# First token block of a retention and ELU layer kernel: whole-chunk products on half arrays, reordered loads, two layer tiles by chunks

## The chip, the cores and the metric

The kernel runs on one core of a Trainium2 chip. The core has a matrix engine, TensorE (PE in the profile, with PEld for its weight loads), three elementwise engines, VectorE (DVE), ScalarE (ACT) and GpSimd (POOL), and a queue engine, SyncE (SP), which issues the DMA transfers here. Each engine works through its own instructions in order, and semaphores tie them together. PE writes into PSUM[...]; everything else lies in SBUF. The metric is the time of one execution on the device in microseconds (us). A profile's span is what lies between the first and the last instruction of the program's own.

## What is computed

```python
gamma = 1.0 - 2.0 ** (-5.0 - np.arange(H))          # H = 8 heads, D = 64, S = 768, B = 4
for t in range(S):
    state = gamma[None, :, None, None] * state + np.einsum('bhd,bhe->bhde', k[:, :, t], v[:, :, t])
    y[:, :, t] = D ** -0.5 * np.einsum('bhd,bhde->bhe', q[:, :, t], state)
x = y.transpose(0, 2, 1, 3).reshape(B * S, H * D)   # 3072 tokens x 512
h = x @ w_in                                        # 512 x 2048
g = np.where(h > 0.0, h, np.exp(np.minimum(h, 0.0)) - 1.0)
out = g @ w_out                                     # 2048 x 512
```

All is fp32. The weights arrive as 64-bit numbers and are turned into fp32 on the chip.

## The kernel before

The 3072 tokens are worked through in six blocks of 512. A block goes through retention (`q`, `k`, `v` to `x`), the first layer with its ELU, and the second layer. Later blocks use a form of Strassen's scheme for both layers; the first block computes its first layer plainly (`plain_first`), because the weights are still arriving.

**Retention.** A block has four chunks of 128 tokens. One load (`load`, 1 MB, L99) brings a chunk: `q` and `k` turned so that channels lie on partitions, and `k` and `v` with tokens on partitions. `scale_v` (L275) multiplies `v` by a power of gamma for each token. Before the change, each chunk is treated as two sub-chunks of 64 tokens: `score_products` (L302) makes `k` times `q` for each sub-chunk and head as 64x64x64 products, which occupy a quarter of the PE array each; a mask on DVE (`mask_pair` L324, or in `scores` L312) cuts them to the causal triangle and stores them over `k`; `state_products` (L332) makes the sum of `k` times `v` of each sub-chunk, and `state_sum` (L343) adds it to the running state; `within` (L389) multiplies the masked scores by `v`; `across` (L399) adds the state times `q`. At the end DVE multiplies by powers of gamma (`etab`, made by ACT in `powers_of`, L246) into the block's input `xb`. The first two chunks are issued one at a time (`outputs_of_first`, L414), the third and fourth as a pair (L1155 to L1166).

**Weights.** Sixteen pieces of 1 MB come in through three staging buffers (`load_piece_parts`, L130). Piece 2n is `w_a[n]`, piece 2n + 1 is `w_b[n]`, for four values of n; the others are the second layer's. `prepare` (L147) reads a piece with ACT: the low words (L164), the top byte (L166), and the high words scaled (L168), unless DVE does this last one (L190). `decode` (L180) then joins them on DVE (L191, L194). A piece can be handled in two halves. When a piece is decoded, `load_piece` issues the load that takes over its buffer. `hold` (L112) makes one load wait for another through a copy of one element on POOL, which the load must follow.

**The layer.** `plain_first` (L489) makes sixteen tiles of 128 features by 512 tokens, four products each. Tiles 4n and 4n + 1 use `w_a[n]`, 4n + 2 and 4n + 3 use `w_b[n]`. Tiles 0 to 4 are made in two halves of 256 tokens, since the second half of `xb` is ready later (tile 0's first half again in two parts of 128); the others in one. They use PSUM banks a, a, b, d in turn, and tile 4 one of the pool that retention uses. Each tile ends in `elu` (L472): two ACT operations (L477, L478) and one on DVE (L481), which is issued one tile later.

**Order.** There is no scheduler: the Python order is the order on each engine. The head of the program, L1108 to L1171, is written out by hand. `unread` (L1104) issues products whose result nothing reads. `take` advances the decoding of the current piece by one step, `next(inner)` issues the next piece of `plain_first`. From L1187 on, a loop over the remaining steps of `plain_first` attaches other work to step n: loads of the next block's chunks, `next_piece` (decode one, prepare the next), the next block's retention from n = 10 on.

Of the kernel before, what the change touches and what calls it, by code (L numbers as in the profile page):

```python
# [18 lines left out]
def kernel(  # L19
# [127 lines left out]
    def prepare(parts=1, by_vector=False, between=None):  # L147

        n = len(prepared)
        if n >= NPIECE:  # L150
            return
        t = staged[n]
        if n < 2 * NQ:
            dst = (w_a, w_b)[n % 2][n // 2].rearrange("p a b c d -> p (a b c d)")
        else:

            dst = w_s[n % NQ].rearrange("p a b c d -> p (a b c d)")[:, 0:1024]
        todo = []
        for part in range(parts):
            if part and between:  # L160
                between()
            c = slice(part * 1024 // parts, (part + 1) * 1024 // parts)
            lo, hi, flat = t[:, c, 0], t[:, c, 1], dst.bitcast(U32)[:, c]
            nc.scalar.activation(flat, lo, AF.Copy, scale=2.0**-29)  # L164
            top = dst.bitcast(F8).rearrange("p (c b) -> p c b", b=4)[:, c, 3]
            nc.scalar.activation(top, hi.bitcast(FP32), AF.Copy, scale=2.0**-120, saturate=False)  # L166
            if not by_vector:
                nc.scalar.activation(lo.bitcast(FP32), hi.bitcast(FP32), AF.Copy, scale=2.0**-112)  # L168
            todo.append((lo, flat, hi if by_vector else None))
        prepared.append((dst, todo))  # L170
# [83 lines left out]
    parts = load_piece_parts(2)  # L254
    next(parts)
    load(1)
    next(parts, None)
    load_piece()
    load(2)
    load(3)  # L260
    load_piece(staged[1][:, :, 0].bitcast(FP32))
# [25 lines left out]
    def state(tb, n):  # L287

        if n % (2 * CPB) == 0:
            return carry[(tb + n // (2 * CPB)) % 2]  # L290
        if (tb, n) == (0, 3):

            return xt[0].rearrange("p a t -> p (a t)")[:, 0:256].rearrange("p (h e) -> p h e", e=D)

        k = raw[tb * CPB + (n - 1) // 2][1][:, 0].rearrange("p h d -> p (h d)")
        return k[:, (n - 1) % 2 * 256 : ((n - 1) % 2 + 1) * 256].rearrange("p (h e) -> p h e", e=D)
# [5 lines left out]
    def score_products(sc, tb, pp, x):  # L302
        qk = raw[tb * CPB + 2 * pp + x][0]
        for p in range(HP):
            for sub in range(2):
                for a in range(2):
                    nc.tensor.matmul(  # L307
                        sc[a][rows(sub), x, p, :], lhsT=qk[rows(a), 1, p, rows(sub)],
                        rhs=qk[rows(a), 0, p, rows(sub)], start=True, stop=True, skip_group_check=True,
                    )  # L310

    def scores(tb, pp):  # L312

        sc = [ps_r.tile([P, 2, HP, D], FP32, name="sc", tag="r") for _ in range(2)]
        for x in range(2):
            score_products(sc, tb, pp, x)
        for a in range(2):
# [4 lines left out]
            )  # L322

    def mask_pair(sc, x):  # L324

        place = raw[x][0][:, 1].rearrange("p h c -> p (h c)").rearrange("p (a n t) -> p a n t", a=2, t=D)
        for a in range(2):
            nc.vector.tensor_tensor(
                out=place[:, a], in0=sc[a][:, x], in1=cmask.unsqueeze(1).to_broadcast([P, HP, D]), op=ALU.mult
            )  # L330
# [12 lines left out]
    def state_sum(kvs, tb, pp, x, sub, copy=None):  # L343
# [3 lines left out]
        if fresh(tb, n):  # L347
            (copy or nc.scalar.copy)(state(tb, n + 1), kvs[sub][:, x])
# [65 lines left out]
    def outputs_of_first():  # L414

        y = [bank(x).rearrange("p a (b x d) -> p (a b) x d", b=2, x=2) for x in "bd"]
        for x in range(2):
            for j in range(4):
                pt = raw[x][0][:, 1].rearrange("p h c -> p (h c)")
                within(0, 0, x, j, y, lambda p: pt[:, ((j // 2) * HP + p) * D :][:, 0:D])  # L420
            yield
            across(0, 0, x, 0, y)
            for sub in range(2):
                if not fresh(0, 2 * x + sub):
                    seen = epool.tile([P, 8], FP32, name="seen", tag="seen")
                    nc.vector.tensor_copy(seen[:, 0:4], y[sub][:, :, x, 0])
            if x:
                yield
            across(0, 0, x, 1, y)
            if x:  # L430
                yield
            for sub in range(2):
                nc.vector.tensor_tensor(
                    out=place_of(xb[:, :, 0 : 2 * C])[:, :, x, sub, :], in0=y[sub][:, :, x],
                    in1=place_of(powers[:, :, 0 : 2 * C])[:, :, x, sub, :], op=ALU.mult,
                )
            if not x:
                yield
# [50 lines left out]
    def plain_first():  # L489
# [12 lines left out]
        for k in range(5):  # L502
            hp = bank("aabd"[k]) if k < 4 else ps_r.tile([P, 2, TH], FP32, name="hp", tag="r")
            banks.append(hp.rearrange("p a b -> p (a b)"))
            if k == 0:
                part(0, slice(0, C))
                yield
                part(0, slice(C, 2 * C))
            else:
                part(k, half[0])  # L510
            if k:
                yield
        for k in range(5):
            part(k, half[1])
            n, w, row, fi = tiles[k]
            elu(g_plain[row * NF + 2 * n + fi], banks[k])
            yield
        for k, (n, w, row, fi) in enumerate(tiles[5:]):
            hp = bank("aabd"[k % 4]).rearrange("p a b -> p (a b)")
# [589 lines left out]
    for n in range(28):  # L1109
# [4 lines left out]
    sc = [ps_r.tile([P, 2, HP, D], FP32, name="sc", tag="r") for _ in range(2)]  # L1114
    score_products(sc, 0, 0, 0)
    scale_v(0)
    mask_pair(sc, 0)
    unread(1, TH)
    kvs = [ps_r.tile([P, 2, HP, D], FP32, name="kv", tag="r") for _ in range(2)]
    state_products(kvs, 0, 0, 0, range(2))  # L1120
    state_sum(kvs, 0, 0, 0, 0, nc.vector.tensor_copy)
    y = outputs_of_first()
    next(y)
    next(y)
    unread(1, TB)
    score_products(sc, 0, 0, 1)
    state_sum(kvs, 0, 0, 0, 1)
    prepare(2, between=lambda: powers_of(slice(2 * C, S)))
    piece = decode(True)
    take()  # L1130
    take()
    scale_v(1)
    mask_pair(sc, 1)
    inner = plain_first()
    next(inner)
    state_products(kvs, 0, 0, 1, range(2))
    state_sum(kvs, 0, 0, 1, 0)
    next(y)
    next(y)
    next(y)  # L1140
    unread(1, TB)
    next(y, None)
    take()
    take()
    take()
    state_sum(kvs, 0, 0, 1, 1)
    prepare(2, by_vector=True)
    next(inner)
    piece = decode()
    take()  # L1150
    take()
    scale_v(2, True)
    scale_v(3, True)
    next(inner)
    scores(0, 1)  # L1155
    states(0, 1)
    take()
    prepare(2)
    piece = decode(True)
    take()  # L1160
    next(inner)
    y = outputs(0, 1)
    next(y)
    next(y)
    take()
    next(y, None)  # L1166
    next(inner)
    take()
    take()
    take()  # L1170
    prepare()  # L1171
# [15 lines left out]
    for n, _ in enumerate(inner):  # L1187
# [4 lines left out]
        if n in (1, 2, 4, 5, 7, 9):  # L1192
            next_piece(n in (1, 2, 5, 7))
# [294 lines left out]
```

## Time and profile before

| what | value |
|---|---|
| time, median of 3 runs | 632.84 us (632.33 to 633.2) |
| time of the profiled execution | 632.87 us |
| its span | 630.9 us |
| PE busy | 624.8 us, 99% |
| DVE busy | 483.1 us, 77% |
| ACT busy | 253.3 us, 40% |
| POOL busy | 21.8 us, 3% |
| mean traffic | 217 GB/s; 403 GB/s from 5.15 to 11.6 us |

A row of the timeline has the start in us, the length in us, engine, line, operation, output and inputs, shape and count, and in brackets how long the engine was idle and what ended that. For PE, 64*64 or 128*128 is the part of the array that is used and 128x512 the output; one fp32 product is two records, so x8 is four products. The ends of PE's records are modelled, so starts are compared. A row of the wait list has who waited for whom, the total in us, how often, and the longest. Chunk loads and piece loads are issued at L110 and L142.

### The profile page before, as it was taken

What the parts mean: (1) busy time and instruction counts of PE and PEld (TensorE: products, weight loads), DVE (VectorE), ACT (ScalarE), POOL (GpSimd) and SP (SyncE); (2) the same over time, 40 slices, a digit from 0 to 9 for tenths busy, and PEclk for the clock granted to TensorE, in tenths of its full rate; (3) what the DMA queues carried; (4) which work ended last, traced back from release to release, by engine and by line L of the source; (5) the groups of instructions that cost most, each with busy time, mean ns of one, the idle gap of its engine ahead of it and who ended that gap; (6) DMA issues with size and microseconds to landing.
All of it is one profiled execution on the core that took longest, in us unless ns stands there. A gap on an engine that the chain in (4) does not pass through costs nothing.

```text
span 630.9 us, 16128 instructions
## 1 busy us (share of the span) xinstructions
PE 624.8 (99%) x6680; PEld 560.1 (89%) x6680; DVE 483.1 (77%) x884; ACT 253.3 (40%) x472; POOL 21.8 (3%) x25
## 2 busy tenths in 40 slices
PE   8999999999999999999999999999999999999998
PEld 5864578888899999889999989999988999988997
DVE  5779789989789675699685588777489877558975
ACT  6698635015541114653112646111465211366311
POOL 1021000000000000200000200000110000000000
PEclk9999999999999999999999999999999999999999
DMA  8698669689287888405888702888810798600794
GB/s 331 278 406 291 188 210 268 196 267 316 81 311 248 239 255 299 180 2 174 274 266 292 282 2 64 264 284 296 310 73 12 216 308 252 217 18 2 232 309 162
DMA packets 75897, 136.85 MB, mean 217 GB/s; under 512 B 6320, under 2 KB 31792, under 8 KB 70704
## 3 DMA queue, kind: packets, MB, share of 16 engines
q1 hardware_dynamic: 75824, 135.82, 64.8%
q8 instruction: 53, 0.87, 0.5%
q14 instruction: 20, 0.16, 0.1%
HBM read 114.56 MB, written 21.23 MB: 215 GB/s over the span
## 4 chain that ended last, share of the span: by engine, by line
PE 77%; SPq 1%; DVE 1%; DMA 1%; issue 0%; ACT 0%; ACTq 0%; DVEq 0%
PE pa L955 20%; PE pa L913 10%; PE pd L955 10%; PE pb L955 5%; PE pa L867 5%; PE pb L913 4%; PE pa L740 4%; PE qa L913 3%; PE pd L867 2%; PE qd L913 2%; PE pd L913 2%; PE pd L740 2%; PE y L394 1%; PE sc L307 1%; PE y L409 1%; PE kv L338 1%
## 5 line engine op out<-in xcount | busy, mean ns | idle before, releaser
L963 ACT COPY ms<-pa 128x128 f32<-128x128 f32 x104 | 27.7, 266 | 146.7 <-PE pa L955 146.7
L955 PE MATMUL pa<-ts,wq 128*128 128x128 f32 x560 | 74.2, 275 | 0.0
L955 PE MATMUL pd<-ts,wq 128*128 128x128 f32 x552 | 73.5, 276 | 0.0
L955 PEld LDWEIGHTS pa<-ts,wq 128*128 128x128 f32 x560 | 68.5, 192 | 0.4
L955 PEld LDWEIGHTS pd<-ts,wq 128*128 128x128 f32 x552 | 67.1, 192 | 0.6 <-DVE res L967 0.2
L955 PE MATMUL pa<-gC,wq 128*128 128x128 f32 x480 | 64.7, 278 | 0.0
L478 ACT ACTIVATE r<-r 128x512 f32<-128x512 f32 x96 | 60.5, 630 | 3.1
L955 PEld LDWEIGHTS pa<-gC,wq 128*128 128x128 f32 x480 | 59.0, 192 | 1.5 <-issue 0.3
L477 ACT ACTIVATE r<-gC 128x512 f32<-128x512 f32 x64 | 39.9, 624 | 32.4 <-DVE gC L921 32.4
L967 DVE TENSOR_TENSOR res<-pd,ms 128x128 f32<-128x128 f32 x68 | 19.5, 287 | 39.6 <-PE pd L955 38.4
L481 DVE SCALAR_TENSOR_TENSOR gC<-r,gC 128x512 f32<-128x512 f32 x64 | 44.0, 719 | 0.7 <-ACT r L478 0.7
L829 DVE TENSOR_TENSOR ts<-gC,ts 128x512 f32<-128x512 f32 x60 | 41.3, 688 | 1.0
L829 DVE TENSOR_TENSOR ts<-gC 128x512 f32<-128x512 f32 x60 | 41.0, 684 | 0.0
L281 POOL TENSOR_TENSOR chunk<-chunk,vf 128x512 f32<-128x512 f32 x16 | 20.0, 1251 | 428.8 <-DMA chunk<-in_qkv_dram 345.8
L955 PE MATMUL pb<-gC,wq 128*128 128x128 f32 x240 | 31.7, 275 | 0.0
L988 ACT COPY res<-pa 128x128 f32<-128x128 f32 x34 | 9.0, 266 | 55.0 <-PE pa L955 55.0
L955 PEld LDWEIGHTS pb<-gC,wq 128*128 128x128 f32 x240 | 29.2, 192 | 0.0
L690 ACT COPY m<-pa 128x512 f32<-128x512 f32 x24 | 13.9, 581 | 30.2 <-PE pa L740 16.3
L921 DVE TENSOR_TENSOR gC<-qa,gC 128x512 f32<-128x512 f32 x8 | 5.5, 692 | 25.0 <-PE qa L913 18.3
L913 PE MATMUL pa<-xt,w_b 128*128 128x256 f32 x96 | 23.0, 382 | 0.0
L913 PE MATMUL pa<-xt,w_s 128*128 128x256 f32 x96 | 23.0, 382 | 0.0
L913 PE MATMUL pa<-xb,w_a 128*128 128x256 f32 x96 | 22.7, 379 | 0.0
(255 smaller groups left out, 1244.3 us busy)
## 6 DMA issues: line engine op xcount, KB each, us to landing
wq<-scratch_dram SPq DMA_DIRECT2D x277, 256.0 KB, 4.3
chunk<-in_qkv_dram SPq DMA_DIRECT2D x23, 1024.0 KB, 8.6
wraw<-in_w_dram SPq DMA_DIRECT2D x15, 1024.0 KB, 6.0
out_dram<-res SPq DMA_DIRECT2D x14, 256.0 KB, 3.8
scratch_dram<-gT SPq DMA_DIRECT2D x12, 256.0 KB, 4.3
scratch_dram<-m SPq DMA_DIRECT2D x12, 192.0 KB, 6.0
scratch_dram<-so SPq DMA_DIRECT2D x4, 512.0 KB, 4.6
scratch_dram<-wi SPq DMA_DIRECT2D x2, 1024.0 KB, 6.4
```

The costliest lines, as they stand in the source:

```text
L281: eng.tensor_tensor(out=kv[:, 1], in0=kv[:, 1], in1=vf[:, i].unsqueeze(2).to_broadcast([C, H, D]), op=ALU.mult)
L477: nc.scalar.activation(e, h, AF.Relu, scale=-1.0)
L478: nc.scalar.activation(e, e, AF.Exp, scale=-1.0)
L481: nc.vector.scalar_tensor_tensor(g, e, -1.0, h, ALU.add, ALU.max)
L690: nc.scalar.copy(m, ps)
L740: nc.tensor.matmul(ps[:, fi, :], lhsT=w[:, fi, j2, :], rhs=x[:, j2, :], start=(begin and fi == 0 and j2 == 0), stop=(j2 == 1), skip_group_ ...
L829: sub = lambda o, x, y: nc.vector.tensor_tensor(out=o, in0=x, in1=y, op=ALU.subtract)
L867: nc.tensor.matmul(ps[:, f, :], lhsT=lhs[f], rhs=xs[j][k], start=(begin and f == 0), stop=True, skip_group_check=True,)
L913: nc.tensor.matmul(ps[:, fi, :], lhsT=w[:, fi, j2, :], rhs=x[:, j2, :], start=(j in (1, 7) and fi == 0 and j2 == 0), stop=(j2 == 1), skip_ ...
L955: nc.tensor.matmul(ps, lhsT=w[:, f, :], rhs=ts[j][k][:, f, :], start=(begin and f == 0), stop=(f == 3), skip_group_check=True,)
L963: nc.scalar.copy(m, ps)
L967: nc.vector.tensor_tensor(out=o, in0=x, in1=y, op=ALU.add)
```

## The change

Four things are different in the first block. The rest of the program is the same, line for line.

- Its four chunks are handled whole. `whole_scores` makes `k` times `q` of 128 by 128 tokens with 64 channels, on the upper or lower half of the array; `whole_mask` masks them against the full triangle on DVE, one mask for each row half, the second result going to a buffer of its own; `whole_products` and `whole_within` contract over all 128 tokens and write 64 rows, on the left or right half of the array; `whole_across` uses quarters, with 128 columns. All four chunks go through the same functions, one at a time, and there is one state per chunk.
- The loads stand in another order: chunk 0 in two halves, chunk 1, piece 0 in two halves, chunks 2 and 3, piece 1, piece 2 (held behind piece 1). Before it was chunk 0 in halves, piece 0's first half, chunk 1, piece 0's second half, piece 1, chunks 2 and 3, piece 2 (held).
- In `plain_first`, tiles 0 and 1 are made in four parts of 128 tokens each, between the chunks' retention; tiles 2 to 15 are made whole. The bank order is a, a, then d, b, a, a in turn.
- The head of the program is written anew. The unread products of 256 and 512 columns between the chunks are gone (the first stays, with 29 small ones instead of 28). Of the weights, pieces 0 and 1 are prepared in the head, in halves, and piece 2 at step n = 0 of the loop; before, pieces 0 to 3 were. POOL scales chunks 2 and 3 instead of DVE. In `prepare`, the scaled high words come second instead of third. The powers for later tokens (`powers_of`, four ACT operations) stand behind both halves of piece 0 instead of between them.

```diff
-    parts = load_piece_parts(2)
-    next(parts)
     load(1)
-    next(parts, None)
-    load_piece()
+    for _ in load_piece_parts(2):
+        pass
     load(2)
     load(3)
-    load_piece(staged[1][:, :, 0].bitcast(FP32))
+    load_piece()
...
+    def whole_scores(m):
+        qk = raw[m][0]
+        sc = [ps_r.tile([P, HP, C], FP32, name="sc", tag="r") for _ in range(2)]
+        for p in range(HP):
+            for a in range(2):
+                nc.tensor.matmul(
+                    sc[a][:, p, :], lhsT=qk[rows(a), 1, p, :], rhs=qk[rows(a), 0, p, :],
+                    start=True, stop=True, skip_group_check=True,
+                )
+        more = hpool.tile([P, TB], FP32, name="pt", tag="h")
+        whole[m] = sc, (qk[:, 1], more.rearrange("p (h c) -> p h c", c=C))
+
+    def whole_mask(m, a):
+        sc, pt = whole[m]
+        nc.vector.tensor_tensor(
+            out=pt[a], in0=sc[a], in1=causal.unsqueeze(1).to_broadcast([P, HP, C]), op=ALU.mult
+        )
+
+    def whole_within(m, y, a):
+        pt, kv = whole[m][1], raw[m][1]
+        for u in range(2):
+            for c in range(2):
+                nc.tensor.matmul(
+                    y[a][rows(c), u, :], lhsT=kv[:, 1, head(a, u, c), :], rhs=pt[a][:, 2 * u + c, :],
+                    start=(u == 0), stop=(m == 0), skip_group_check=True,
+                )
+
+    def whole_across(m, y, a):
+        q = raw[m][0]
+        for u in range(2):
+            for c in range(2):
+                p = 2 * u + c
+                nc.tensor.matmul(
+                    y[a][rows(c), u, :], lhsT=state(0, 2 * m)[rows(a), p, :], rhs=q[rows(a), 0, p, :],
+                    start=False, stop=True, skip_group_check=True,
+                )
+
+    def whole_products(m):
+        kv = raw[m][1]
+        t = ps_r.tile([P, HP, D], FP32, name="kv", tag="r")
+        for p in range(HP):
+            for a in range(2):
+                nc.tensor.matmul(
+                    t[rows(a), p, :], lhsT=kv[:, 0, 2 * p + a, :], rhs=kv[:, 1, 2 * p + a, :],
+                    start=True, stop=True, skip_group_check=True,
+                )
+        return t
+
+    def whole_sum(m, t):
+        if m:
+            nc.vector.tensor_tensor(out=state(0, 2 * m + 2), in0=t, in1=state(0, 2 * m), op=ALU.add)
+        else:
+            nc.scalar.copy(state(0, 2), t)
+
+    def whole_end(m, y, a):
+        c, j = slice(m * C, (m + 1) * C), slice(2 * a, 2 * a + 2)
+        nc.vector.tensor_tensor(out=xb[:, j, c], in0=y[a], in1=powers[:, j, c], op=ALU.mult)
+
+    def whole_outputs(m):
+        y = whole_place()
+        for a in range(2):
+            whole_within(m, y, a)
+            if m:
+                whole_across(m, y, a)
+        return y
...
-        for k in range(5):
-            hp = bank("aabd"[k]) if k < 4 else ps_r.tile([P, 2, TH], FP32, name="hp", tag="r")
...
+        for k in range(2):
+            banks.append(bank("a").rearrange("p a b -> p (a b)"))
+            for x in range(2):
+                part(k, slice(x * C, (x + 1) * C))
                 yield
...
+        for x in (2, 3):
+            for k in range(2):
+                part(k, slice(x * C, (x + 1) * C))
+                if x == 3:
+                    n, w, row, fi = tiles[k]
+                    elu(g_plain[row * NF + 2 * n + fi], banks[k])
                 yield
...
-    for n in range(28):
+    for n in range(29):
...
+    whole_scores(0)
     scale_v(0)
-    mask_pair(sc, 0)
...
+    whole_mask(0, 0)
+    whole_mask(0, 1)
+    scale_v(2)
+    scale_v(3)
+    load_piece(staged[1][:, :, 0].bitcast(FP32))
+    t = whole_products(0)
+    whole_sum(0, t)
+    y = whole_outputs(0)
+    whole_end(0, y, 0)
+    whole_end(0, y, 1)
+    whole_scores(1)
+    prepare(2)
+    piece = decode(True)
+    scale_v(1)
+    whole_mask(1, 0)
+    whole_mask(1, 1)
+    y = whole_outputs(1)
+    t = whole_products(1)
+    whole_end(1, y, 0)
     take()
     take()
+    whole_end(1, y, 1)
+    whole_sum(1, t)
     inner = plain_first()
     next(inner)
+    powers_of(slice(2 * C, S))
+    whole_scores(2)
     next(inner)
+    take(3)
+    whole_mask(2, 0)
+    whole_mask(2, 1)
     next(inner)
+    y = whole_outputs(2)
+    t = whole_products(2)
+    whole_end(2, y, 0)
+    whole_end(2, y, 1)
+    whole_sum(2, t)
+    whole_scores(3)
+    next(inner)
+    whole_mask(3, 0)
+    whole_mask(3, 1)
     prepare(2)
     piece = decode(True)
+    y = whole_outputs(3)
     next(inner)
+    whole_end(3, y, 0)
+    whole_end(3, y, 1)
+    t = whole_products(3)
     next(inner)
+    whole_sum(3, t)
+    take(2)
...
-        if n in (1, 2, 4, 5, 7, 9):
-            next_piece(n in (1, 2, 5, 7))
+        if n == 0:
+            take(3)
+            prepare(2)
+        elif n in (1, 2, 3, 4, 5, 7, 9):
+            next_piece(n in (2, 3, 5, 7))
```

## The prediction

> **What bounds the kernel now.** First the page's busy line, then the wait list of TensorE (PE) for the first 95 us, then the timeline of PE and of whatever released it there.
>
> ```profile
> PE 624.8 (99%) x6680; PEld 560.1 (89%) x6680; DVE 483.1 (77%) x884; ACT 253.3 (40%) x472; POOL 21.8 (3%) x25
> ```
>
> ```profile
> PE pa L1106 <- DVE blank L208: 1.5, 1, 1.5
> PE pd L409 <- DVE seen L426: 0.5, 2, 0.3
> PE kv L338 <- DVE chunk L281: 0.4, 1, 0.4
> PE y L409 <- DVE seen L378: 0.3, 1, 0.3
> PE pa L497 <- DVE w_a L194: 0.2, 1, 0.2
> ```
>
> PE is the bound nearly everywhere: 99% of the span, and after the first 28 us this list has no entry; the same list from 86 us to the end is empty. So what the front of the kernel gains or loses in PE time reaches the end whole, and one number measures it: when the first tile that both kernels issue alike starts. That is tile 5 of the plain layer, the first row of the two below that has 512 columns.
>
> ```profile
> 15.92 3.10 PE L497 MATMUL pa<-xb,w_a 128*128 128x128 f32 x16
> ...
> 20.86 1.16 PE L307 MATMUL sc<-chunk 64*64 64x64 f32 x64
> 21.84 1.11 PE L338 MATMUL kv<-chunk 64*64 64x64 f32 x64
> 22.88 1.99 PE L497 MATMUL pd<-xb,w_b 128*128 128x256 f32 x8
> ...
> 38.21 2.31 PE L521 MATMUL pa<-xb,w_a 128*128 128x512 f32 x5
> 41.65 3.60 PE L521 MATMUL pa<-xb,w_b 128*128 128x512 f32 x8
> 45.08 3.60 PE L521 MATMUL pb<-xb,w_b 128*128 128x512 f32 x8
> ...
> 60.93 3.70 PE L521 MATMUL pb<-xb,w_b 128*128 128x512 f32 x8
> 64.56 2.08 PE L338 MATMUL kv<-chunk 64*64 64x64 f32 x112
> ```
>
> Tile 5 starts at 38.21. From 15.92 on PE runs without a hole; before that it waits for loads and fills itself with products that nothing reads (L1106). Loads land one after the other, and these rows show when:
>
> ```profile
> 8.11 0.68 ACT L164 ACTIVATE w_a<-wraw 128x512 uint32<-128x512 uint32 x1 [2.33 <-DMA wraw<-in_w_dram]
> 10.66 0.56 PEld L307 LDWEIGHTS sc<-chunk 64*64 64x64 f32 x32 [0.85 <-DMA chunk<-in_qkv_dram]
> 15.10 0.17 POOL L115 COPY wraw<-wraw 1x1 f32<-1x1 f32 x1 [12.83 <-DMA wraw<-in_w_dram]
> ```
>
> By place in the SP queue these are the loads that complete 1.5, 2.5 and 4 MB.
>
> **What the Trainium skill says.** "TensorEngine Tiling (Array Packing)", Key Properties: tiles of one mode run side by side, and "Mode switching requires drain". The trace agrees with both. Sixteen 64x64 products with 64 columns start at 12.65 and the next group at 13.16 (0.51 us): four at a time, since one 128-column product on the whole array takes 0.223 (groups of four start at 321.15, 322.05, 322.94). A 512-column tile takes 3.43 among its like (41.65 to 45.08) and 3.63 between two 64x64 groups (60.93 to 64.56): 0.20 for going in and out. The same page lists 64x128 and 128x64 as modes of two tiles; no run here shows either. "TensorE: Matmul & The Clock Gate", Part 1: the array starts at half clock and is released after some 3.4 us of activity. The trace shows it: 32 records of scores take 0.99 (5.15 to 6.14), 32 records of state 0.51 (12.65 to 13.16).
>
> **The change, part by part.** (a) Unread products: four become one large at the start; those at 6.14, 9.51 and 14.96 go (0.9 to 1.1 each). They fill waits, so taking them away gives nothing by itself.
>
> (b) Retention of four chunks. Before, each of its four products per chunk is sixteen 64x64x64 products, 0.47 to 0.51, so about 2.0 per chunk. After, per chunk: scores, eight 64x128 products of 128 columns; within, eight 128x64 of 128 columns; across, eight 64x64 of 128 columns with only the two column halves alternating, so two at a time; state, eight 128x64 of 64 columns. If two run at a time: scores 4 x 0.223 = 0.89, within 0.89, across 0.89, state 0.46 (the present price of 16 products in fours). That is 3.13, 1.1 more per chunk: half of each causal square is computed and masked away. An unseen price is whether pairs run side by side: bounded by 0.89 (all) and 1.79 (none) for scores; I take all, since 64x64 tiles that share rows or columns do it now.
>
> (c) Mode changes. Before, the second pair of chunks costs three excursions. After, within and across alternate for each half array, so a chunk changes mode six or seven times. Price of one segment: 0.20 for a full-array one (above); 64x64 ones with 32 or 64 records show 0.05 to 0.17 over 0.0145 per record (20.86 to 21.84 is 0.98 for 64, that is 0.05; 21.84 to 22.88 is 0.11). I take 0.15 per half-form segment and 0.13 for across; the bounds are 0 and 0.20.
>
> (d) Layer tiles. Five tiles by halves become two by chunks and three whole: the same columns. A 128-column product costs 0.223, so a tile 3.57 instead of 3.43: +0.28 for two.
>
> (e) Loads. Chunk 1 moves ahead of the first weight piece, and chunks 2 and 3 ahead of the second. By megabytes: chunk 0 as now (scores start at 5.15); chunk 1 completes 2 MB, between 8.11 and 10.66, so 9.4; the halves of piece 0 at 2.5 and 3 MB, 10.66 and about 12.6 (ACT takes up the second half of piece 0, now also at 3 MB, at 12.58); chunk 2 at 4 MB, 15.1; chunk 3 at 5 MB, 17.6; piece 1 at 6 MB, about 20.2. Piece 2 is held by the POOL copy until piece 1 is there; from issue to landing takes some 4.8 with the queue empty, so 25.2. SP issues the next load behind it, and POOL has the two scalings in front: neither late.
>
> **The walk.** Chunk 0: scores 5.15 to 6.7 (half clock until about 6.3), scale on DVE 6.46 to 7.15, masks (0.6 apart) done 7.75 and 8.35, products behind them done by 9.0. Chunk 1 lands at 9.4: scores to 10.4, result in DVE 10.55, first mask 11.2. Then on PE within, across, within, across (0.45 + 0.14 each, 2.36), state 0.61: 14.2. The first part of tile 0 needs the first half of piece 0: ACT 10.66 to 12.7, DVE behind the first end of chunk 1 (12.9) with 0.42 and 0.70: 14.05, just in time. Part 0: 1.06 (as 11.59 to 12.65 now): 15.3. Chunk 2 is there (15.1). From here PE has everything: scores 1.04; two parts 1.99; within/across twice 2.36; state 0.61; scores 1.04; part 1.09; within/across 2.36; part 1.09; state 0.61; three parts 2.78; tiles 2 to 4, 3 x 3.43 = 10.3. The sum is 25.3, so tile 5 starts at 40.6: 2.4 later than now. The part of tile 0 that waits longest, its last, needs both ends of chunk 3, some 2 us old by then.
>
> What could be late behind it: piece 1 is prepared by ACT 20.2 to 24, but DVE's decode stands behind the last state sum, about 28.1, two operations 1.1 for the first half: 29.2, and PE wants it at 30.3. ACT then does piece 2 (six operations, 3.8 by 22.79 to 26.61) between the ELUs of tiles 0 and 1 (1.17 each), 30.8 to 34.6, decoded 35.4, tile 4 wants it at 37.1. Piece 3 (3.5) moves behind that, so ELUs run late: adding 2.4 or 3.5 for each of pieces 4 to 6, tile 5's leaves ACT at 52.4 and DVE at 53.1, and its bank is wanted by tile 9 at 54.3. The cover is 1 us or more each time; were it gone, PE would wait for the remainder. DVE masks eight arrays of 512 columns (0.6 each) instead of four of 256 and two of 512: 2 us more, in the stretch where PE is 5 us longer. After tile 5 the order is the same.
>
> Sum against the profiled execution: span 630.9 + 2.4 = 633.3; its time 632.87 lies 0.03 above the median, so 632.84 + 2.4 = 635.2.
>
> **Rivals.** (1) Mode changes between half forms cost nothing: the twelve half-form segments after 15.3 carry 1.7 of overhead in my sum; without it tile 5 starts at 38.9, 0.7 later: 633.5, not slower than can be told. For it: some 64x64 groups follow each other at 0.05. Against: 0.20 at every full-array segment. It decides from 0.05 per segment down. Measurement tells 0.2% (1.3 us) from no change.
>
> (2) Halves don't run side by side. Row halves alone: scores of chunks 1 to 3 +0.89 each, 2.7: 637.9. Column halves alone: within +0.89 each and state +0.46 each, chunks 1 to 3, 4.1: 639.3. For it: no row of the profile has such a pair; against: quarters do it.
>
> (3) The clock falls back: without the unread products PE idles between 6.7 and 11.2 for about half the time. One window of 3.4 us (the skill's page above) at half rate is 1.7: 636.9. Against: the granted clock is at its highest digit in every slice, and 10.04 to 10.66 is idle today without harm.
>
> (4) Faster: needs tile 5 before 36.9, 3.7 off my sum, more than all overhead in it; a residue.
>
> **Chances and range.** Mine 0.62, (1) 0.18, (2) 0.12, (3) 0.05, (4) 0.03. The likeliest's own range is 634.0 to 636.5, from 0.05 to 0.25 per segment and 0.5 for the landing of chunk 2. The wide range runs from 633.3, leaving out (4) and part of (1), to 638.0, which holds (3) and the row halves. Slower by over 0.2%: 0.76, mine less its lowest tenth and with (2) and (3); within: 0.20; faster: 0.04.
>
> **What would show it.** Right: scores in groups of 16 records taking about 0.9 to 1.0; tile 5 at 40 to 41; an empty PE wait list after 15 us; the span longer by what tile 5 is late. Groups of 1.8 mean (2). Step times of 0.2 per 128-column record in a stretch after 7 us mean (3). Wrong altogether if PE waits for an ELU's bank at tiles 9 or 10, or for weights at tile 2, or if tile 5 starts before 38.2.

## The result, and the profile after

The changed kernel takes 638.48 us (median of 4 runs, 637.77 to 640.25), against 632.76 for the kernel before on the same chip: a ratio of 1.0095, with an interval of 1.0073 to 1.0116. It is slower, as forecast, but by 5.7 us and not by 2.4, and lies 0.5 above the range. Its profiled execution took 638.45, with a span of 636.2. That is 5.3 us of span more than before, and 0.3 more outside the span (638.45 less 636.18 is 2.27; before, 632.87 less 630.90 was 1.97).

The busy line of the page, and the whole wait list of PE:

```profile
PE 627.4 (99%) x6420; PEld 558.6 (88%) x6420; DVE 481.5 (76%) x874; ACT 254.7 (40%) x475; POOL 21.9 (3%) x27
```

```profile
PE pa L1129 <- DVE blank L206: 1.5, 1, 1.5
PE pa L763 <- DVE m L618: 1.1, 1, 1.1
PE kv L439 <- DVE chunk L277: 0.9, 1, 0.9
PE pb L419 <- DVE chunk L411: 0.8, 1, 0.8
PE pa L544 <- DVE gC L508: 0.7, 1, 0.7
PE pa L763 <- ACT m L713: 0.5, 1, 0.5
PE sc L402 <- DMA chunk<-in_qkv_dram: 0.4, 1, 0.4
```

PE is still busy 99% of the span, with 260 records fewer. But three entries of the list (L763 twice, L544) lie behind tile 5, where before there was none. The timeline of PE says where. All starts are in us; the wait of a row is in its brackets.

```profile
9.04 1.16 PE L402 MATMUL sc<-chunk 64*128 64x128 f32 x16
...
15.52 1.16 PE L402 MATMUL sc<-chunk 64*128 64x128 f32 x16 [0.39 <-DMA chunk<-in_qkv_dram]
...
18.60 0.66 PE L419 MATMUL pb<-chunk 128*64 128x128 f32 x8
19.18 0.65 PE L429 MATMUL pb<-chunk 64*64 64x128 f32 x8
19.77 0.66 PE L419 MATMUL pd<-pt,chunk 128*64 128x128 f32 x8
...
30.56 3.60 PE L544 MATMUL pd<-xb,w_b 128*128 128x512 f32 x8
...
37.43 7.03 PE L544 MATMUL pa<-xb,w_a 128*128 128x512 f32 x16
...
51.99 4.56 PE L544 MATMUL pa<-xb,w_a 128*128 128x512 f32 x10 [0.67 <-DVE gC L508]
...
138.39 1.99 PE L763 MATMUL pa<-xt,w_a 128*128 128x256 f32 x8 [1.10 <-DVE m L618]
```

The row at 37.43 holds tiles 4 and 5; tile 5's first record starts at 40.87. How late PE is against the kernel before at the same instruction, stage by stage:

| PE instruction | before | after | late by | new here |
|---|---|---|---|---|
| tile 5 | 38.21 | 40.87 | 2.66 | 2.66 |
| tile 8 | 48.51 | 51.99 | 3.48 | 0.82 |
| second layer begins | 85.20 | 88.78 | 3.58 | 0.10 |
| next block's first layer | 133.54 | 138.39 | 4.85 | 1.27 |
| its fifth product | 140.71 | 146.08 | 5.37 | 0.52 |
| last PE row | 627.64 | 632.90 | 5.26 | -0.11 |

So half of the loss is the front that the prediction had worked out. The other half arises behind it, at tile 8 and at the next block's first layer. In the kernel before, PE has no wait at these places:

```profile
48.51 3.60 PE L521 MATMUL pd<-xb,w_a 128*128 128x512 f32 x8
...
133.54 1.89 PE L740 MATMUL pa<-xt,w_a 128*128 128x256 f32 x8
...
140.71 1.99 PE L740 MATMUL pa<-xb,w_b 128*128 128x256 f32 x8
```

The rows of VectorE at both places, after the change; the first three show where tile 4's last ELU operation (L508) comes, the last is where the later loss begins:

```profile
48.48 0.68 DVE L563 TENSOR_TENSOR h<-gC,gC 128x512 f32<-128x512 f32 x1
...
50.65 0.69 DVE L563 TENSOR_TENSOR h<-gC,h 128x512 f32<-128x512 f32 x1
51.26 0.68 DVE L508 SCALAR_TENSOR_TENSOR gC<-r,pa 128x512 f32<-128x512 f32 x1
...
99.48 0.56 DVE L670 TENSOR_TENSOR m<-w_s 128x384 f32<-128x384 f32 x1 [1.28 <-DMA scratch_dram<-m]
```

And the last of each before:

```profile
48.34 0.68 DVE L481 SCALAR_TENSOR_TENSOR gC<-r,hp 128x512 f32<-128x512 f32 x1
...
94.54 0.55 DVE L647 TENSOR_TENSOR m<-w_s 128x384 f32<-128x384 f32 x1
```

**Tile 8.** It takes the bank (a PSUM buffer of 512 fp32 columns) of tile 4. ACT had finished tile 4's exponential at 47.81 (L505), and VectorE was busy with a decode until 48.5, so it could have released the bank at 49.2. It did so at 51.9, because the four subtractions of `inputs_of_first` (L563), issued at n = 4, stand in front of the ELU's last operation in VectorE's queue. Before, they stood there too, from 45.57 to 48.4, but tile 4 was in a bank of the retention pool (`hp` in the row above), for which no tile waited.

**The small sums.** Four small sums (L670) reuse buffers that a store must have read. VectorE reached them at 98.2 and waited 1.28. Up to 137 it has no slack in which to catch up. Its one long gap there, 2.00 at 137.05 for a store of `gT`, was 1.95 before; that store comes behind VectorE's own results and is as late as they are. So VectorE is 5.37 late when it releases the bank that PE needs at 138.39. Before, the same sum started at 94.54 with no gap, the store having landed at 94.49: 0.05 of cover.

### The profile page after: what moved, and what is told of

The parts are those of the page before. It is cut to its first block, busy times and chain, and to the rows that moved or that the text cites. A ratio compares the mean times of both kernels' runs of the same rounds, so it can differ in the third digit from the quotient of the medians.

```text
span 636.2 us, 15626 instructions
## 1 busy us (share of the span) xinstructions
PE 627.4 (99%) x6420; PEld 558.6 (88%) x6420; DVE 481.5 (76%) x874; ACT 254.7 (40%) x475; POOL 21.9 (3%) x27
## 4 chain that ended last, share of the span: by engine, by line
PE 77%; SPq 1%; DVE 1%; DMA 1%; issue 0%; ACT 0%; ACTq 0%; DVEq 0%
PE pa L978 20%; PE pa L936 10%; PE pd L978 10%; PE pb L978 5%; PE pa L890 5%; PE pb L936 4%; PE pa L763 4%; PE qa L936 3%; PE pd L890 2%; PE qd L936 2%; PE pd L936 2%; PE pd L763 2%; PE y L375 1%; PE sc L302 1%; PE y L390 1%; PE kv L319 1%
## 5 line engine op out<-in xcount | busy, mean ns | idle before, releaser
L505 ACT ACTIVATE r<-r 128x512 f32<-128x512 f32 x96 | 60.5, 630 | 3.1
L508 DVE SCALAR_TENSOR_TENSOR gC<-r,gC 128x512 f32<-128x512 f32 x64 | 43.1, 706 | 0.7 <-ACT r L505 0.7
L277 POOL TENSOR_TENSOR chunk<-chunk,vf 128x512 f32<-128x512 f32 x18 | 20.2, 1122 | 444.8 <-DMA chunk<-in_qkv_dram 240.6
```

Of the source, the lines that this page charges most:

```text
L277: eng.tensor_tensor(out=kv[:, 1], in0=kv[:, 1], in1=vf[:, i].unsqueeze(2).to_broadcast([C, H, D]), op=ALU.mult)
L505: nc.scalar.activation(e, e, AF.Exp, scale=-1.0)
L508: nc.vector.scalar_tensor_tensor(g, e, -1.0, h, ALU.add, ALU.max)
```

## The experiments

"Late by" is always against the kernel before at the same instruction (of PE, unless VectorE is named), in profiled executions, one for each version. The kernel before ran beside each group: 633.5, 633.8 and 633.9 us on those chips. The intervals of many versions overlap, so the single terms are read from the profiles and not from the times.

**The changed kernel again**, unaltered, beside the next three.

> The changed kernel once more, unaltered, for a second profile and for the same chip as the runs beside it. If the three terms read from the first profile (2.65 us of work in front of tile 5, 0.8 us of waiting for the bank of tile 8, 1.3 us in which VectorE waits for the store of its small sums at 98 us, and what follows from that) belong to the change, all three stand here again within 0.3 us, at about 638.4 us. If the third is a matter of how one execution's transfers happened to fall, it is between 0 and 2 us here and the time differs by as much.

638.15 us (636.35 to 641.02), ratio 1.0057 (1.0028 to 1.0086). The trace has the same steps: tile 5 late by 2.08, tile 8 by 2.93, second layer 3.03, next block 4.51, end 4.90. The front is 0.58 shorter than in the first profile, where 0.3 was expected: the scores of chunk 2 start at 14.95 and don't wait for their load, where they had started at 15.52. Tile 8 adds 0.85 (0.82), the next block 1.48 (1.27).

**Shift: does being late cost more than itself?** The kernel before, with four more unread products of 512 columns ahead of tile 0's second half.

```diff
-    unread(1, TB)
+    unread(5, TB)
```

> The kernel before with four more unread products of 512 columns ahead of the second half of tile 0, 4 x 0.86 = 3.4 us of TensorE time and nothing else. Theory A, that work put in front is added to the end and no more: tile 5 starts 3.4 us later and the time is 636.2 us. Theory B, that a front that is 3.4 us late is enough to bring on the later waits (VectorE for its stores at 98 us, TensorE for VectorE at 138 us): 637.5 to 638.2 us, with those waits in the lists.

636.66 us, ratio 1.0047 (1.0033 to 1.0062). Of 3.43 us put in, 2.59 arrive at tile 5 (the rest fills waits). Tile 9 waits for a bank (0.4 on PE's list), and then PE is late by 3.25 at the second layer and by 3.25 at the next block: the 1.27 doesn't appear. VectorE finds the store landed. So being late by as much as the changed kernel does not bring the loss at 138. Something else did. The end is late by 4.30 all the same: ahead of 225.06 PE stands for 0.53 with no wait but "issue", which is time for which the profile shows no reason, and from there it is late by 3.99, from 303.6 by 4.31. Such holes come back below.

**Bank: the four subtractions one step later** (n = 5 instead of 4), which puts tile 4's ELU ahead of them.

```diff
+        if n == 5:
+            run(inputs_of_first(0, [hslot() for _ in range(3)]))
...
-        if n == 4:
-            run(inputs_of_first(0, [hslot() for _ in range(3)]))
-        elif n == 10:
+        if n == 10:
```

> The changed kernel with one edit: the four subtractions that make the second layer's first inputs move on VectorE from step 4 to step 5 of the loop, so that the last operation of tile 4's ELU stands ahead of them and frees tile 8's bank 2.8 us earlier. Theory A, the order on VectorE makes TensorE wait at tile 8: that wait (0.7 to 0.8 us) is gone and the time is 0.8 lower, 637.6. Theory B, ScalarE's lateness makes it wait: the wait stays, since ScalarE does the same. Theory C, a later wait that doesn't depend on this one eats the gain: the wait is gone and the time stays at 638.4.

637.06 us, ratio 1.0046 (1.0035 to 1.0058). The list of PE from 5 us on:

```profile
PE pa L763 <- DVE m L618: 1.1, 1, 1.1
PE pb L419 <- DVE chunk L411: 1.0, 2, 0.8
PE pa L763 <- ACT m L713: 0.5, 1, 0.5
```

The wait for L508 is gone: tile 8 starts at 51.10, late by 2.59 as tile 5 is, and the end is late by 4.40 instead of 5.26 (4.90 in again). Both waits at L763 stay. The four operations ahead of tile 4's ELU are the cause of the loss at tile 8, and the loss at the next block doesn't depend on it.

**Across: within and across over all four halves in turn.** In the change, one half array's within and across alternate with the other's; here all of within comes first, then across with its row halves alternating as well.

```diff
+    def whole_across(m, y):
...
+            for a in range(2):
+                for c in range(2):
...
+        if m:
+            whole_across(m, y)
```

> The changed kernel with the products of state and q issued after both row halves of the masked products and with row and column halves alternating, so four 64x64 tiles at a time and two mode changes fewer in a chunk. By my prices 0.45 + 2 x 0.145 = 0.74 us less per chunk; chunks 2 and 3 pass it on, chunk 1 waits for chunk 2's load anyway. Theory A: tile 2 starts 1.5 us earlier (29.1), the time is 1.5 lower, 636.9. Theory B, mode changes cost nothing here and only the four at a time count: 0.9 lower, 637.5. Theory C, ScalarE and VectorE set the pace behind tile 2 whatever TensorE does: tile 2 earlier, but the wait at tile 8 longer by as much and the time the same.

Tile 5 starts at 39.52, 1.35 earlier than in the changed kernel's first profile and 0.77 earlier than in again; end late by 2.88. The median, 637.09, ratio 1.0055 (1.0042 to 1.0068), is over the profiled 636.15, so that the times alone would not show the gain. From within of chunk 2 to its state products it takes 1.62 us (18.67 to 20.29) instead of 2.34 (18.60 to 20.94): both arrays' across take 0.6 together instead of 1.17, since quarters that differ in both halves run four at a time, and two segments of within in a row follow at 0.49 instead of 0.58, without the change of mode. Three chunks save 1.9 on PE; a wait for piece 0 (L525 for DVE's `w_a` L192, 1.1) takes more than half of it back. VectorE waits only 0.23 at the small sums here, and PE is idle for only 0.04 at the next block's first layer.

**Smalls: taking the store's wait away by order.** VectorE's remaining sum of the pieces is put ahead of the small sums.

```diff
             smalls = small_of_pieces(1)
-            some(smalls, 4)
             run(parts)
             run(smalls)
```

> The changed kernel, with the second half of the sums of pieces 10 and 11 taken ahead of the first four small sums on VectorE, so that these find the earlier store from their buffers landed. Theory A: the 1.28 us that VectorE waits for that store at 99.5 us is what makes PE wait at 138 us (1.1 us). Without it VectorE is some 4.0 late at 137 and PE 3.6, within the margin of about 0.5 that the kernel before has there: no wait of PE for VectorE at 138, a span of 634.7 to 635.1, a profiled time near 637, and a ratio near 1.003. Theory B: VectorE is late there by its own work, and the store is only one of the things it waits for: the wait at 138 stays near 1 us and the span at 635.8 to 636.2.

638.93 us, 1.0083 (1.0059 to 1.0107); next block late by 5.11. The edit failed to do what it was for: VectorE still waits 0.98 for the store, since that landed as late as ever, and then 0.51 for ACT. It tells neither theory from the other. **Both** (bank_smalls, 638.98 us, 1.0070 with 1.0047 to 1.0093) has the same fault, and **three** adds across:

> The changed kernel with both small edits: the four subtractions one step later, and the second half of the sums ahead of the small sums. Theory A: what the change costs is three terms that add, 2.6 at the front of PE, 0.7 to 0.8 for the bank of tile 4, 1.1 to 1.3 behind the store. With the last two gone the span is 2.6 to 3.1 over that of the kernel before: 633.5 to 634.0, a profiled time near 635.9, ratio about 1.003 less than that of the changed kernel. Theory B: the terms overlap, one wait hides in another, and the span stays at 634.6 or more, as with one edit alone.

> As the run with both small edits, and within and across of all four tiles in turn instead of one by one (three segments fewer per chunk). Theory A: the front loses another 1.3 us (tile 5 near 39.5), the span is 632.3 to 632.9, within 2 us of the kernel before, and nothing else waits. Theory B: the shorter front only exposes other waits (for the weights of tile 2 or a bank of the ELU), and the span stays over 633.2.

Three: 636.82 us, 1.0044 (1.0030 to 1.0059), span 635.0; tile 5 at 39.49 as expected, 0.34 and 0.51 at L764 (L763 of the changed kernel), and a hole that nobody had expected: 1.21 us at 303.50 in the middle of a row of L390, put down to "issue". Bank_smalls has a hole of the same length at 305.39. More on it below.

**Loads: the load order undone** in the changed kernel.

> The changed kernel with the loads in the order of before: the first half of piece 0 ahead of chunk 1, piece 1 ahead of chunks 2 and 3. Theory A: PE waits for chunk 2, which now completes 5 MB (17.6 us) instead of 4 MB (15.1): the scores of chunk 2 start near 18.0 instead of 15.5, tile 5 near 43.3, and the span is 638.3 to 638.8, the profiled time near 640.5. Theory B: chunk 2 isn't what binds, since VectorE and the weights of the first tile are as late: tile 5 stays within 1 us of 40.9 and the span under 637.2.

642.94 us, 1.0143 (1.0121 to 1.0166). The row of chunk 2's scores:

```profile
17.49 1.16 PE L403 MATMUL sc<-chunk 64*128 64x128 f32 x16 [0.92 <-DMA chunk<-in_qkv_dram]
```

Chunk 2 binds here, as theory A had it: scores 1.97 later, tile 5 at 42.83, 1.96 later. The rest (span 640.2 instead of 638.3 to 638.8) is another hole of issue, 1.8 us at L391. The new load order is a part of the change that helps it.

**What is different when the store lands late?** The trace gives sixteen landing times for each store, one for each share, and the start of every packet of instructions (queue 8, 16 KB, about 1 us each). That these are PE's is inferred: there are 53 in the kernel before and in shift and 51 in the changed kernel, which has 260 PE records and as many weight loads fewer. For the first store of small sums, in microseconds after the first share landed:

```
kernel        instruction packet   15th, 16th share   VectorE   PE at
              between 90 and 99    landed             waits     L763/L740
before        none                 1.03  1.16         0         0
shift         none                 0.75  0.77         0         0
after         96.34                0.84  2.21         1.28      1.10
again         95.77                0.78  2.39         1.49      1.31
bank          95.28                0.75  2.26         1.26      1.09
loads         98.17                0.94  2.26         1.27      1.1
across        93.90                0.81  1.24         0.23      0.04
three         93.23                0.82  1.15         0         0.34
```

One share of sixteen is 1.3 to 1.6 behind the fifteenth wherever an instruction packet starts 0.2 to 0.5 us before the store ahead of this one begins to land (also in smalls and bank_smalls), 0.3 to 0.4 behind where the packet is a microsecond earlier (across, three), and 0.0 to 0.1 where there is none (before, shift). Shift has its packet at 87.70, the kernel before at 86.57. So a new theory P: the change removes 260 PE records, so the fetches of PE's instructions fall at other places in its work, and one falls on this store. (Theory Q, its rival: the longer front shifts VectorE against the queue.) It can be tried with no change to the work: more or fewer of the small unread products that fill the wait for the first chunk.

**Phase: the changed kernel with 30 PE records more at the start**, in the same time.

```diff
-    unread(1, TB)
-    for n in range(29):
+    unread(1, TH)
+    for n in range(44):
```

> The changed kernel with 30 records of TensorE more ahead of its first scores, in the same time (an unread product of 256 columns instead of 512, and 44 small ones instead of 29), so that its fetches fall 30 records earlier: the one at 96.34 us moves to about 90. Theory P: all sixteen shares of the store land within 1.3 us of each other, the wait of VectorE at 99.5 (1.28 us) goes or is under 0.3, that of TensorE at 138 (1.1) is under 0.4, and the span is 634.5 to 635.3. Theory Q: both waits stay and the span is 635.6 to 636.4.

From 92 to 99 us the page of the DMA queues has this line for the changed kernel, and no line of queue 8 for phase:

```profile
q8 instruction: 1, 0.02, 0.9%
```

The packet is now at 86.04, the sixteen shares land within 0.80, VectorE has no wait at the small sums (they start at 98.19), and PE none at 138: late by 3.66 ahead of it and behind it. That is what P said of the place. But the span is 636.2, where Q had it, and the time 638.92 (1.0080, 1.0058 to 1.0102): in PE's list of phase there is another entry, and it costs what was gained.

```profile
PE y L390 <- issue: 1.1, 1, 1.1
```

**Bank_phase**, both edits:

> As the run with 30 records more, and the four subtractions one step later. Theory P: what is left is the front of TensorE, 2.6 us at tile 5, and at most 0.5 at 143: span 633.5 to 634.3, unless an instruction fetch comes too late for TensorE elsewhere, which would show as a wait for issue. Theory Q: the wait at 138 stays and the span is 634.9 or more.

Tile 5 late by 2.74, tile 8 by 2.74, next block 2.87; then 0.51 at the fifth product (which follows an ELU input of VectorE, L718) and 0.3 of issue at 223. End late by 3.92. The losses at tile 8 and at the next block's first product are gone, as theory P has it; the span, 634.8, is 0.5 over its figure and 0.1 under Q's. The median, 637.84 with runs from 636.42 to 642.45, ratio 1.0068 (1.0039 to 1.0097), is too scattered to show it.

**Best**, with across as well:

> All of it: within and across of four tiles in turn, the four subtractions one step later, 30 records more at the start. Theory P: tile 5 near 39.5, nothing else late but up to 0.5 at 143: span 632.2 to 632.9, 1.3 to 2 us over the kernel before; no part of the change is left that gains on it. Theory Q: 633.2 or more.

637.29 us, 1.0051 (1.0030 to 1.0072). Next block late by 1.72 only, but then 2.43 us of issue at 224.19; end late by 4.68, and the span, 635.6, is again over P's figure. No version tried beats the kernel before.

**Before_phase: the kernel before with 28 PE records fewer at the start**, and one unread product of 224 columns to fill the time.

```diff
     unread(1, TB)
-    for n in range(28):
+    unread(1, 224)
+    for n in range(13):
```

> The kernel before with 28 records of TensorE fewer ahead of its first scores (13 small unread products instead of 28, and one unread product of 224 columns to fill the same time). Nothing behind the first scores is different, but TensorE's instruction fetches fall 28 records later: the one at 86.57 us moves to about 92.6, onto the stores of the sums, where the changed kernel has one. Theory P (the fetch makes one of the sixteen shares of the store late): that share lands some 1.3 us behind the others, VectorE waits 1.0 to 1.4 us for it at 94.5, TensorE waits 0.6 to 1.2 at 133.5, and the span grows by 0.7 to 1.7 us, to 631.6 to 632.6, with no change in retention or layer. Theory Q (VectorE waits because the front shifts VectorE against the queue): the shares land together as before and the span stays at 630.7 to 631.2.

638.13 us, ratio 1.0069 (1.0047 to 1.0092): 4.2 us lost, with nothing changed but fillers that nobody reads. Not mainly by the expected path, though, and the span, 635.8, is over both theories' figures. The packet went to 98.72, not 92.6, behind the first stores, and their shares land within 0.92. For the most part PE itself stands with no wait but issue. Its timeline:

```profile
25.44 0.79 PE L394 MATMUL y<-chunk 64*64 64x64 f32 x34
27.91 0.63 PE L394 MATMUL y<-chunk 64*64 64x64 f32 x27 [1.68 <-issue]
...
80.07 0.27 PE L409 MATMUL y<-chunk 64*64 64x64 f32 x2 [0.76 <-issue]
```

A group of 64 records stops after 34. An instruction packet ran from 25.51 to 26.53, and PE went on 1.4 us after its end. At 80.07 the packet had ended at 78.59, 1.5 before; in phase the hole ends 1.4 after its packet (223.33 and 224.75). A third hole of 0.6 follows at 325.86; of the 4.9 us by which PE ends late, 0.3 was there ahead of the hole at 25 us. In the kernel before, the packets of that stretch start at 22.65 and 26.36 and PE has no hole.

The expected path is there as well, one group of stores later. The store that begins to land at 99.44, 0.7 behind the packet at 98.72, has its last share 0.81 behind the fifteenth (0.07 for the same store before), and VectorE waits for it:

```profile
101.28 0.69 DVE L647 TENSOR_TENSOR gT<-so 128x512 f32<-128x512 f32 x1 [0.42 <-DMA scratch_dram<-gT]
```

VectorE's lateness goes from 3.39 to 4.08 there, and PE's from 3.32 at the second layer to 4.13 at the fifth product of the next block.

**All traces together.** In the 14 traces, 483 transfers (of those whose shares land within 4 us) begin to land less than 1 us after an instruction packet starts. Their last share is 0.75 behind the fifteenth in the median, and more than 0.7 in 53% of them. For the other 5046 the median is 0.17, and 13% are over 0.7. So a packet makes a late share much more frequent, but not every packet does it, and it isn't the only thing that does.

**VectorE in all versions.** How late VectorE and PE are, by the time of the same instruction in the kernel before:

| version | VectorE, 93.93 (ahead of the small sums) | VectorE, 99.38 (behind them) | VectorE, 116.35 (behind three decodes) | VectorE, 138.17 (`h`) | PE, 133.54 (next block) | PE, 140.71 (fifth product) |
|---|---|---|---|---|---|---|
| after | 3.57 | 4.98 | 5.32 | 5.37 | 4.85 | 5.37 |
| across | 2.28 | 2.65 | 2.99 | 3.02 | 2.50 | 3.02 |
| phase | 3.65 | 3.59 | 3.93 | 3.99 | 3.66 | 3.98 |
| best | 1.71 | 1.70 | 2.05 | 2.06 | 1.72 | 2.06 |
| shift | 3.24 | 3.27 | 3.30 | 3.32 | 3.25 | 3.32 |
| before_phase | 3.32 | 4.08 | 4.09 | 4.13 | 3.61 | 4.13 |

At the fifth product PE is as late as VectorE, within 0.01, in every trace; at the next block's first product it is 0.52 less late than VectorE, or as late as PE itself already was. So the 1.27 and the 0.52 are one loss, VectorE's, at two places with different cover. Part of it, 0.34 in after, across, phase and best, arises in three decodes, and not in shift and before_phase. One of them, after and before:

```profile
104.96 0.69 DVE L189 TENSOR_SCALAR wraw<-wraw 128x1024 uint32<-128x1024 uint32 x1
105.80 1.23 DVE L192 CUSTOM_DVE_ANT_0 w_s<-wraw,w_s 128x2048 uint16<-128x2048 uint16 x1
...
99.98 0.69 DVE L191 TENSOR_SCALAR wraw<-wraw 128x1024 uint32<-128x1024 uint32 x1
100.71 1.22 DVE L194 CUSTOM_DVE_ANT_0 w_s<-wraw,w_s 128x2048 uint16<-128x2048 uint16 x1
```

The second operation comes 0.84 behind the first instead of 0.73: the idle time between them is 0.14 instead of 0.03. At all three decodes (105.80, 115.53, 120.34) the trace has an instruction of VectorE in between that waits, so that the second operation has a wait for ACT's semaphore beside that for VectorE's own; at the same three before (100.71, 110.31, 115.02) it has VectorE's own alone. This fits the new order in `prepare`: the top byte, which the second operation reads, is now ACT's last result, where before the first operation's wait for ACT covered it. No run undoes the order, so this cause is argued and not shown.

## Why the prediction was right or wrong

**The bound and the walk** were right. PE is the bound, what the front loses reaches the end, and tile 5 came at 40.87 for 40.6 (40.29 in again). Term by term: scores 1.10 each for 1.04, within and across 0.58 and 0.59 a segment for 0.59 and 0.58, state 0.61 for 0.61, the parts of layer tiles 1.09 for 1.09, chunk 2's scores at 15.52 for 15.3, tile 2 at 30.56 for 30.3. That the binding stretch starts so near the figure is in part luck: PE's own work would have let the scores start at about 15.1, earlier than worked out, and the load of chunk 2 came 0.4 later than worked out. (The reading that PE before has no hole from 15.92 on leaves out 0.26 at 27.09, which changes nothing.) The loads show as these rows, for 9.4, 10.66, 15.1 and 20.2:

```profile
9.04 0.97 PEld L402 LDWEIGHTS sc<-chunk 64*128 64x128 f32 x16 [0.24 <-DMA chunk<-in_qkv_dram]
...
20.46 0.17 POOL L115 COPY wraw<-wraw 1x1 f32<-1x1 f32 x1 [1.40 <-DMA wraw<-in_w_dram]
```

The other two are ACT's first half at 10.30 and the scores at 15.52 above.

**The rivals.** Mode changes do cost: a segment of within takes 0.58 with a change behind it and 0.49 without one (across), so about 0.1 each, and some 0.04 more is there without a change; that is the 0.14 of the sum, but a third of it isn't the mode (rival 1 falls). Halves do run side by side: 16 records of 64x128 in 1.10 (rival 2 falls). That agrees with the Trainium skill, "TensorEngine Tiling (Array Packing)", Key Properties, that different tiles execute in parallel, now also in the two modes that no row of the kernel before had shown. After its idle stretches PE is no slower: a segment of within takes 0.59 at 11.02, right behind 0.8 of waiting, and 0.58 at 18.60 (rival 3 falls). The page's clock digit doesn't decide this: it is 9 in the first slice too, where PE's first products before ran at half the later rate (32 records of scores in 0.99, 32 of state in 0.51). And nothing gained (rival 4). Of the signs that the prediction gave, tile 5 came as said, but the wait list behind 15 us is not empty, and PE waits for the bank of an ELU, at tile 8 and not at 9 or 10.

**What failed** is the paragraph "What could be late behind it", in two sentences. The first is "The cover is 1 us or more each time". It followed tile 5's bank to tile 9 along ACT, where the cover was there. It did not follow tile 4's bank to tile 8, which the new bank order had joined, and on VectorE it left out the four subtractions in front of the ELU: 0.82, shown by bank, where it goes.

The second is "After tile 5 the order is the same". That is nearly true, and no argument: the order is the same, but the places where PE's instructions are fetched are not, and VectorE's waits in the decodes are not. A fetch that falls on the store of the small sums comes with a late share, and VectorE waits for it, in a chain that had 0.05 us of cover. Phase, bank_phase and best take the packet away and with it that wait, and before_phase brings one on at another store. But all four miss theory P's span, because PE's own holes move too, so that it is the waits at these places that speak for P, in one profile each. How a packet delays a share stays open, since the trace doesn't say which DMA engine carries a packet. VectorE becomes 1.37 later at the first small sum, and 0.34 in the decodes; with 0.08 of small differences that is 1.79, which PE meets as 1.27 at the next block and 0.52 at its fifth product.

The sum "632.84 + 2.4" also took the time outside the span as unchanged. It grew by 0.3: 2.26 to 2.36 in the profiled executions of all versions of the changed kernel, 1.91 to 2.02 in those of the kernel before, shift and before_phase, for a reason that no run shows.

The sum that holds is then 2.66 (front) + 0.82 (tile 8) + 0.10 (its second product, behind the wait) + 1.79 (VectorE) - 0.11 = 5.26 on PE, and 0.3 outside.

## What to carry to other kernels

Where an engine is the bound with no idle time, a new order is paid for twice: by its own length, and by every place downstream where the old order happened to be just in time. Follow each buffer that changes hands through the queues of all engines that release it, counting everything that stands in front of the releasing instruction, and look for chains with a cover of nearly nothing before calling the rest of a program unaffected. And count instructions: a change in the number of PE instructions moves the instruction fetches of everything behind it. In one try in this kernel that was worth nearly as much as the change itself (4.2 us for fillers against 5.7), so a comparison of two versions that differ in their count contains that too.

## What the runs showed of the hardware that was not expected

- PE can stand with no wait that the profile shows, a microsecond and more after an instruction packet. Eleven such holes in eight traces, of 0.3 to 2.4 us, lie in groups of 64x64 products (some 15 ns a record) or, twice, just behind one (shift at 225.06, before_phase at 325.86), and all end 1.2 to 1.5 us after a 16 KB packet of queue 8 had ended. Twenty-eight records fewer at the start cost 4.2 us of 633.9.
- A store counts as landed with the last of its sixteen shares (99.45, and VectorE goes on at 99.48). An instruction packet among the data packets goes with a late last share: 1.3 to 1.6 us in six kernels at the small sums, 0.75 in the median over all traces against 0.17 without one.
- Pairs of half-array tiles keep pace with quarters: a 128-column record of 64x128 or 128x64 takes 55 to 56 ns where two run side by side, and of 64x64, with all four quarters in turn, about 27. Quarters of which only the column half alternates take 55, two at a time.
